# Two attentions on one core: one of four integer patterns moved from VectorE to an accumulating DMA

## The chip, the cores and the metric

The kernel runs on one core of one Trainium2 chip. The metric is the device time of one execution in microseconds, the median of several. PE is TensorE, ACT ScalarE, DVE VectorE, POOL GpSimd and SP SyncE. A run's "granted clock" is the mean share of full speed that TensorE's clock was given. PSUM is the memory that TensorE writes its results to.

## The reference, cut to what matters

```python
def _A_ref(x, wq, wk, wv, wo, beta):       # S = 2048, D = 512, 32 heads of 16, 4 segments of 512
    ...
    for s in range(N):
        logits = einsum('bhqd,bhkd->bhqk', qs, ks) * scale + mask      # causal within the segment
        a_dot = einsum('bhqk,bhkd->bhqd', softmax(logits), vs)
        ...                                                            # plus a memory read, gated
def _B_ref(x, wqkv, wo):                                               # plain attention over all 2048
    scores = einsum('bhqd,bhkd->bhqk', q, k) * Dh ** -0.5
    return einsum('bhqk,bhkd->bhqd', softmax(scores), v) ... @ wo
return concatenate([a, b], axis=-1)
```

B alone has 32 x 2048 x 2048 exponentials; they are the bulk of the work.

## The kernel before

The program is written by a planner in Python. It keeps a clock for each engine and decides, step by step, what TensorE does next; the order that comes out is fixed in the program. Exponentials are made in two ways. ScalarE takes score tiles of two or three banks of 512 columns out of PSUM (`pT`). VectorE takes whole quads: four 128x512 score tiles (four heads, one key block of B). It writes them as 16-bit integers which, read as fp16, are a rough exponential; three more copies with other offsets (the `LADDER`) even out the error, and TensorE adds the four patterns in PSUM.

```python
LADDER = (12914, 13046, 13325, 13628)
VBUFS = 11          # buffers of 128x2048 uint16
VBACK = 1.5         # us of VectorE backlog up to which a score tile for VectorE is added
...
        def v_evac(u, kb, x, j, vt, end):            # first pattern, four times a quad
            def f():
                pin(nc.vector.tensor_scalar(x[:, j, :], vt[:], XSCALE, float(LADDER[0]), ALU.mult, ALU.add))
                if end:
                    buf = [len(LADDER)]
                    v_ready(u, kb, x, buf)
                    for off in LADDER[1:]:
                        later(0.70, v_rung(u, kb, x, off, buf), ...)      # cut
            return f

        def v_rung(u, kb, x, off, buf, pool=False):  # one further pattern, three times a quad
            def f():
                vlive[0] += 1
                p = wk.tile([P, 4, 512], U16, name="vx", tag="vx", bufs=VBUFS)
                ...                                                       # cut
                pin(nc.vector.tensor_scalar(p[:], x[:], float(off - LADDER[0]), 32767.0, ALU.add, ALU.min))
                v_ready(u, kb, p, [1], ...)
                v_done(buf)
            return f
```

ScalarE always takes the next tile; a quad goes to VectorE when buffers, PSUM slots and the backlog allow. So the number of quads is a result of the planning, and ScalarE's number of tiles is what remains.

## Time and profile before

| | before |
|---|---|
| time, median | 897.12 us at the prediction, 897.05 us with one more run |
| profiled span | 893.6 us (of a run of 895.34 us), granted clock 0.996 |
| ACT / PE / DVE busy | 869.0 / 862.0 / 794.3 us |
| exponentials on ACT | 374 of three banks, 375 of two |
| quads on VectorE | 124 (496 evacuations, 372 offsets) |

A group's line in the profile gives the source line, engine, operation, what it writes and reads with shapes, the count, then busy us and mean ns of one, then the idle time of the engine before it and what ended that. The prediction shows the lines of before. Busy time is the union of intervals, so where consecutive instructions overlap, as on ScalarE, it is less than count times mean.

### The profile page before, as it was taken

The numbers are of one execution on the slowest core, as the hardware profiler recorded it, in microseconds if no ns is written. First come the engines' busy times: TensorE is split into PE (matmuls) and PEld (weight loads), VectorE is DVE, ScalarE is ACT, GpSimd is POOL, SyncE is SP. The second block draws the span as 40 slices with busy tenths as digits, with TensorE's granted clock in tenths as the row PEclk, the third lists the DMA queues.
The fourth block names the chain that finished last, engine by engine and source line by source line (L and its number), as shares of the span: only waits on it lengthen the run. The fifth ranks groups of instructions, "written<-read, shape, count | busy, mean of one in ns | idle before, by whom it ended". The sixth has DMA issues, their size and how long they took to land.

```text
span 893.6 us, 18889 instructions
## 1 busy us (share of the span) xinstructions
PE 862.0 (96%) x7659; PEld 258.0 (29%) x7659; DVE 794.3 (89%) x1355; ACT 869.0 (97%) x779; POOL 156.5 (18%) x333
## 2 busy tenths in 40 slices
PE   9999999999999999999999999999999999999996
PEld 3322222332223222232222332223233222222222
DVE  4787689899898897989899998999999999999996
ACT  6999999999999999999999999999999999999995
POOL 5711210430303012040220303003030300000000
PEclk9999999999999999999999999999999999999999
DMA  9400100110002110000000110000000000000000
GB/s 194 89 15 11 67 4 6 30 30 2 5 3 43 37 24 8 1 1 7 2 7 1 47 32 1 2 2 1 1 1 1 7 25 19 1 2 1 1 1 29
DMA packets 42801, 17.05 MB, mean 19 GB/s; under 512 B 34512, under 2 KB 42704, under 8 KB 42704
## 3 DMA queue, kind: packets, MB, share of 16 engines
q1 hardware_dynamic: 41360, 15.23, 7.3%
q8 instruction: 62, 1.02, 0.5%
q10 hardware_dynamic: 1344, 0.52, 0.2%
q14 instruction: 35, 0.29, 0.1%
HBM read 4.20 MB, written 4.19 MB: 9 GB/s over the span
## 4 chain that ended last, share of the span: by engine, by line
PE 28%; ACT 15%; issue 6%; DVE 4%; POOL 1%; ACTq 0%; POOLq 0%
PE acc L117 15%; ACT pT L892 15%; PE s_ps L117 7%; PE v_ps L117 4%; DVE vx L965 1%; DVE vx L981 1%; POOL pT L902 1%; PE o_ps L117 1%; DVE tT L374 0%; PE l_ps L117 0%; PE k_ps L117 0%; ACT ex L299 0%; POOL qB L274 0%; DVE osb L1264 0%; PE q_ps L117 0%
## 5 line engine op out<-in xcount | busy, mean ns | idle before, releaser
L892 ACT ACTIVATE pT<-s_ps 128x1536 bf16<-128x1536 f32 x749 | 856.9, 1286 | 7.2 <-PE s_ps L117 5.4
L965 DVE TENSOR_SCALAR vx<-v_ps 128x512 uint16<-128x512 f32 x496 | 322.9, 682 | 28.4 <-PE v_ps L117 23.6
L117 PE MATMUL s_ps<-qB,KB 32*128 32x512 bf16 x1552 | 251.8, 383 | 10.4 <-ACT pT L892 7.1
L981 DVE TENSOR_SCALAR vx<-vx 128x2048 uint16<-128x2048 uint16 x372 | 244.6, 690 | 4.5 <-PE acc L117 2.6
L117 PE MATMUL acc<-vx,VB 128*32 128x512 f16 x1984 | 178.0, 384 | 1.1 <-DVE vx L981 0.5
L117 PE MATMUL v_ps<-qB,KB 32*128 32x512 bf16 x496 | 175.8, 381 | 2.8 <-DVE KB L253 0.9
L902 POOL TENSOR_SCALAR_AFFINE_SELECT pT<-pT 128x256 bf16<-128x256 bf16 (+2 forms) x241 | 105.7, 473 | 359.4 <-ACT pT L892 358.5
L117 PEld LDWEIGHTS <-KB 32*128 32x128 bf16 x2048 | 83.4, 91 | 245.8 <-issue 238.3
L117 PE MATMUL acc<-pT,VB 128*32 128x512 bf16 x1552 | 151.2, 388 | 0.2 <-DVE tT L374 0.2
L117 PE MATMUL acc<-zeros 128*128 128x512 bf16 x395 | 133.6, 387 | 0.0
L117 PEld LDWEIGHTS <-VB 128*32 128x32 bf16 x3536 | 73.0, 94 | 155.3 <-issue 142.6
L117 PEld LDWEIGHTS <-zeros 128*128 128x128 bf16 x415 | 34.1, 98 | 83.9 <-issue 77.0
L117 PE MATMUL s_ps<-qA,kA 32*128 32x384 bf16 (+3 forms) x512 | 52.6, 299 | 5.0 <-ACT pT L892 2.8
L374 DVE STREAM_TRANSPOSE tT<-acc 128x512 f32<-128x512 f32 x64 | 45.0, 704 | 10.9 <-PE acc L117 10.7
L274 POOL TENSOR_SCALAR qA<-qc,par 128x512 bf16<-128x512 bf16 x24 | 17.4, 739 | 178.7 <-DVE qc L272 178.7
L117 PE MATMUL acc<-pT,vA 128*32 128x256 bf16 (+3 forms) x512 | 32.8, 306 | 1.5 <-DVE vx L965 1.1
L117 PEld LDWEIGHTS <-kA 32*128 32x128 bf16 x512 | 17.7, 91 | 46.1 <-issue 43.3
L454 DVE CAST osb<-o_ps 128x512 bf16<-128x512 f32 x28 | 19.2, 684 | 9.9 <-PE o_ps L117 9.9
L274 POOL TENSOR_SCALAR qB<-qc,par 128x512 bf16<-128x512 bf16 x32 | 23.7, 754 | 11.8 <-DVE qc L272 11.8
L408 POOL TENSOR_TENSOR tN<-tT,rsum 128x512 bf16<-128x512 f32 x1 | 1.4, 1372 | 129.8 <-DVE rsum L397 129.8
L272 DVE CAST qc<-q_ps 128x512 bf16<-128x512 f32 x28 | 19.0, 680 | 2.8 <-PE q_ps L117 2.6
L117 PE MATMUL v_ps<-w_a,xT_a 128*128 128x512 bf16 x64 | 19.3, 384 | 0.3 <-DVE vx L965 0.2
(93 smaller groups left out, 431.6 us busy)
## 6 DMA issues: line engine op xcount, KB each, us to landing
out_dram<-osb SPq DMA_DIRECT2D x30, 128.0 KB, 1.7
w_b<-in_B_wqkv_dram SPq DMA_DIRECT2D x3, 512.0 KB, 6.0
phk<-phkT SPq DMA_TRANSPOSE x48, 2.4
w_a<-in_A_wv_dram SPq DMA_DIRECT2D x1, 512.0 KB, 4.9
wo_a<-in_A_wo_dram SPq DMA_DIRECT2D x1, 512.0 KB, 4.3
wo_b<-in_B_wo_dram SPq DMA_DIRECT2D x1, 512.0 KB, 5.1
xT_b<-in_B_x_dram SPq DMA_TRANSPOSE x28, 3.3
xT_a<-in_A_x_dram SPq DMA_TRANSPOSE x16, 2.8
```

The lines of the kernel that those rows point to most:

```text
L117: return pin(nc.tensor.matmul(out, lhsT, rhs, **k))
L272: pin(nc.vector.tensor_copy(qc[:], ps[:]))
L274: pin(nc.gpsimd.tensor_scalar(dst[:, e, :], qc[:], par[:, e:e + 1], 0.0, ALU.mult, ALU.add))
L374: pin(nc.vector.transpose(st["tT"][:, e].rearrange("p c d -> p (c d)"), acc[:]))
L408: pin(eng.tensor_tensor(o, tT[:, :, :, 0:DH], rr.to_broadcast(bc), op=ALU.mult))
L454: pin(nc.vector.tensor_copy(osb[:], ps[:]))
L892: pin(nc.scalar.activation(pT[:, 0:n, :], pt[:, 0:n, :], ACT.Exp, scale=SCALE))
L902: pin(nc.gpsimd.affine_select(out=blk, in_=blk, compare_op=ALU.is_ge, fill=0.0, base=0, pattern=[[0, len(sls)], [1, P]], channel_multiplie ...
L965: pin(nc.vector.tensor_scalar(x[:, j, :], vt[:], XSCALE, float(LADDER[0]), ALU.mult, ALU.add))
L981: pin(nc.vector.tensor_scalar(p[:], x[:], float(off - LADDER[0]), 32767.0, ALU.add, ALU.min))
```

## The change

The intent: the fourth pattern is the first plus a constant, so after TensorE has used the first pattern and VectorE has made the two others from it, a DMA can add the constant to the first pattern's buffer in place. That takes a third of the offsets from VectorE, and a quad needs one buffer fewer. GpSimd issues the DMA. At the same time there is one buffer more, and a lower backlog limit, and projections of a segment of A are held until the x tiles should have landed.

```diff
-VBUFS = 11
+VBUFS = 12
-VBACK = 1.5
+VBACK = 1.0
+DMARUNG = 3
+ACCPOOL = 1.05
+ACCDMA = 3.0
+ACCLAT = 3.2
+FILL = 2048
...
+        fill = wk.tile([P, 1, FILL], U16, name="fill")
+        nc.gpsimd.memset(fill[:], LADDER[DMARUNG] - LADDER[0])
...
                     chore(d - LEAD, part(q()), 4, after=rel if s else ARRIVE["w1" if rt == 1 else "wq"],
-                          key=("q", "a", s, rt))
+                          key=("q", "a", s, rt), ok=lambda: s in xTA)
...
+                    for c in chores:
+                        if c["key"] in [(w, "a", s, r) for w in "kq" for r in range(NRT)]:
+                            c["after"] = T["sp"] + 4.0
...
-                    buf = [len(LADDER)]
+                    buf = [len(LADDER) - 1, u, kb, x]
...
-                    for off in LADDER[1:]:
-                        later(0.70, v_rung(u, kb, x, off, buf), ...)
+                    for i in range(1, len(LADDER)):
+                        if i != DMARUNG:
+                            later(0.70, v_rung(u, kb, x, LADDER[i], buf), ...)
...
+        def v_sum(u, kb, x):
+            def f():
+                pin(nc.gpsimd.dma_start(out=x[:].rearrange("p j c -> p (j c)").rearrange("p (a c) -> p a c", c=FILL),
+                                        in_=fill[:].to_broadcast([P, 2048 // FILL, FILL]), accum_op=ALU.add))
+                T["dma"] = max(T["dma"], T["pool"]) + ACCDMA
+                v_ready(u, kb, x, [1], T["dma"] + ACCLAT)
+            return f
...
         def v_done(buf):
             buf[0] -= 1
-            vlive[0] -= buf[0] == 0
+            if buf[0] == 0 and len(buf) > 1:
+                atasks.append((max(T["pe"] + PELAT, T["dve"]), v_sum(*buf[1:])))
+            else:
+                vlive[0] -= buf[0] == 0
```

Cut: an unused way to put offsets on GpSimd is removed, the projection of A's keys gets a like condition, `v_done` is called after a pattern's products instead of before them, and the planner's loops drain the waiting sums.

More of the change, by code (lines that the diff above doesn't have):

```diff
@@ L58 @@
 VALONE = 1.4
-POOLMIN = 99
+DMARUNG = 3
[3 more added lines that the diff above has]
+FILL = 2048
 SPLOADS = 38.0
@@ L97, in pin @@
         return tc.keep_in_program_order(ins)
-    T = dict(pe=0.0, act=0.0, dve=0.0, pool=0.0, sp=SPLOADS)
+    T = dict(pe=0.0, act=0.0, dve=0.0, pool=0.0, sp=SPLOADS, dma=0.0)
     group = dict(kind=None, pos=set(), start=0.0, end=0.0)
@@ L138, in on_pool, with later @@
         ports["pool"].append((start, T["pool"]))
-    def later(us, f, src=None, prio=0, ready=None, ok=None, port=False, rung=None):
+    def later(us, f, src=None, prio=0, ready=None, ok=None, port=False):
         if not live[0]:
@@ L146, in later @@
         seq[0] += 1
-        tasks.append(dict(prio=prio, seq=seq[0], ready=ready, us=us, f=f, src=src, ok=ok, port=port, rung=rung))
+        tasks.append(dict(prio=prio, seq=seq[0], ready=ready, us=us, f=f, src=src, ok=ok, port=port))
     def palloc(pool, shape, name):
@@ L578, in project @@
                     chore(d - LEAD, part(k()), 4, after=rel if s else ARRIVE["w1" if rt == 1 else "wk"],
-                          key=("k", "a", s, rt), ok=lambda: s == 0 or ("phk", s - 1, rt) in seen)
+                          key=("k", "a", s, rt), ok=lambda: s == 0 or s in xTA and ("phk", s - 1, rt) in seen)
                     chore(d - LEAD, part(q()), 4, after=rel if s else ARRIVE["w1" if rt == 1 else "wq"],
-                          key=("q", "a", s, rt))
+                          key=("q", "a", s, rt), ok=lambda: s in xTA)
                 if rt == 0:
@@ L687 @@
         held.update(pk=0, ph=0)
-        vlive, npool = [5], [0]
+        vlive = [5]
         def begin(t):
@@ L727, in backlog @@
             return max(0.0, T["dve"] - T["pe"]) + sum(t["us"] for t in runnable() if t["ready"] < T["pe"] + 0.6)
-        ptasks = deque()
+        ptasks, atasks = deque(), deque()
         def in_turn(g, prio, end=None):
@@ L812, in urge @@
             if dve_force():
+                return
+            if atasks:
+                T["pe"] = group["end"] = max(T["pe"], atasks[0][0])
+                pool_run()
                 return
@@ L966, in f, with v_rung @@
                 if end:
-                    buf = [len(LADDER)]
+                    buf = [len(LADDER) - 1, u, kb, x]
                     v_ready(u, kb, x, buf)
-                    for off in LADDER[1:]:
-                        later(0.70, v_rung(u, kb, x, off, buf), prio=2, ready=T["dve"], ok=lambda: vlive[0] < VBUFS,
-                              port=True, rung=v_rung(u, kb, x, off, buf, True) if off == LADDER[1] else None)
+                    for i in range(1, len(LADDER)):
+                        if i != DMARUNG:
+                            later(0.70, v_rung(u, kb, x, LADDER[i], buf), prio=2, ready=T["dve"],
+                                  ok=lambda: vlive[0] < VBUFS, port=True)
             return f
-        def v_rung(u, kb, x, off, buf, pool=False):
+        def v_rung(u, kb, x, off, buf):
             def f():
@@ L977, in f @@
                 p = wk.tile([P, 4, 512], U16, name="vx", tag="vx", bufs=VBUFS)
-                if pool:
-                    pin(nc.gpsimd.tensor_scalar(p[:], x[:], 1.0, float(off - LADDER[0]), ALU.mult, ALU.add))
-                else:
-                    pin(nc.vector.tensor_scalar(p[:], x[:], float(off - LADDER[0]), 32767.0, ALU.add, ALU.min))
-                v_ready(u, kb, p, [1], T["pool"] + 0.4 if pool else None)
-                v_done(buf)
+                pin(nc.vector.tensor_scalar(p[:], x[:], float(off - LADDER[0]), 32767.0, ALU.add, ALU.min))
+                v_ready(u, kb, p, [1])
+                v_done(buf)
+            return f
[5 more added lines that the diff above has]
+                v_ready(u, kb, x, [1], T["dma"] + ACCLAT)
             return f
@@ L993, in pool_run @@
                 f()
-            while T["pool"] < T["pe"] + 0.1:
-                el = [t for t in runnable() if t["rung"] is not None and t["ready"] < T["pe"] + 0.1]
-                if not el or backlog() < POOLMIN:
-                    return
-                t = min(el, key=lambda t: t["seq"])
-                tasks.remove(t)
-                on_pool(2.15, max(T["pe"], t["ready"]))
-                npool[0] += 1
-                t["rung"]()
+            while atasks and (atasks[0][0] < T["pe"] + 0.1 or not live[0]):
+                ready, f = atasks.popleft()
+                T["pool"] = max(T["pool"], ready) + ACCPOOL
+                f()
         def v_ready(u, kb, p, buf, at=None):
@@ L1085, in pv @@
                 pvq.remove(q)
-                if "v" in q:
-                    v_done(q["v"])
                 at = q["ready"]
@@ L1104, in pv @@
                        tile_position=(0, 32 * j), skip_group_check=True)
+                if "v" in q:
+                    v_done(q["v"])
                 if stop:
@@ L1207 @@
                 urge()
-        while chores or cur_chore[0] or tasks or ptasks or len({q["u"]["id"] for q in pvq}) > 1:
+        while chores or cur_chore[0] or tasks or ptasks or atasks or len({q["u"]["id"] for q in pvq}) > 1:
             dve_run(T["pe"])
@@ L1236 @@
             partial(sb, t())
-        while pvq:
+        while pvq or atasks:
+            pool_run()
             assert pv(1, True)
```

## The prediction

> **What bounds the kernel now.** I read the page first (busy shares, then the slices), then the costliest groups, then the waits, then the stretches of time, and last the timeline of the end. The page's busy shares and the slices of PE, DVE and ACT:
>
> ```profile
> PE 862.0 (96%) x7659; PEld 258.0 (29%) x7659; DVE 794.3 (89%) x1355; ACT 869.0 (97%) x779; POOL 156.5 (18%) x333
> ...
> DVE  4787689899898897989899998999999999999996
> ACT  6999999999999999999999999999999999999995
> POOL 5711210430303012040220303003030300000000
> ```
>
> Both ACT and PE look full, but they are not full in the same way. The scores are turned into exponentials on two engines. ACT does it exactly. VectorE takes whole key blocks ("quads" of four 128x512 tiles), evacuates the four as integers (first pattern) and adds three offsets; TensorE sums the four patterns. The costliest groups (operation, tiles, count, then busy us, mean ns of one, idle before):
>
> ```profile
> L892 ACT ACTIVATE pT<-s_ps 128x1536 bf16<-128x1536 f32 x374 | 560.0, 1497 | 7.2 <-PE s_ps L117 5.4
> L892 ACT ACTIVATE pT<-s_ps 128x1024 bf16<-128x1024 f32 x375 | 403.3, 1076 | 0.0
> L965 DVE TENSOR_SCALAR vx<-v_ps 128x512 uint16<-128x512 f32 x496 | 322.9, 682 | 28.4 <-PE v_ps L117 23.6 <-PE s_ps L117 1.6
> L981 DVE TENSOR_SCALAR vx<-vx 128x2048 uint16<-128x2048 uint16 x372 | 244.6, 690 | 4.5 <-PE acc L117 2.6 <-PE v_ps L117 0.3
> L117 PE MATMUL acc<-zeros 128*128 128x512 bf16 x395 | 133.6, 387 | 0.0
> ```
>
> ACT lost only 7.2 us before all its 749 exponentials. PE's 862 us contain 133.6 us of multiplications by zeros, which the schedule puts in where PE would otherwise be idle. So PE has slack that the busy share hides, and ACT has none. The waits say it from the other side: PE waits for ACT more than ACT for PE, and no PE instruction is listed as waiting for an x transfer:
>
> ```profile
> PE s_ps L117 <- ACT pT L892: 9.9, 41, 0.6
> ...
> ACT pT L892 <- PE s_ps L117: 5.4, 15, 0.9
> ```
>
> The busy times of 45 to 880 us (PE, PEld, DVE, ACT, POOL):
>
> ```profile
> 45.00:880.00 835.00, 812.97 (x7291) 241.55 (x7290) 761.72 (x1296) 829.14 (x741) 125.64 (x248) 1.00 0.05 12
> ```
>
> ACT was idle 835.0 - 829.1 = 5.9 us there. The remaining 24.6 - 5.9 = 18.7 us of its idle time lie in the head and in the tail, which no faster VectorE shortens. The kernel is bound by the number of exponentials on ACT; VectorE matters through how many quads it takes from ACT.
>
> **What the Trainium skill says.** First, "DMA: Bandwidth & Descriptors", section "SWDGE vs HWDGE vs iDMA": an accumulating DMA has to be issued from GpSimd, whose cores write the descriptors into SBUF, and VectorE's two-port modes can lock GpSimd out meanwhile. "SBUF — State Buffer", section "Who interferes with whom", names tensor_scalar among the operations that enter those modes, and says that data movement itself does not contend with an engine. The trace of before has no DMA from GpSimd, so it cannot confirm either. Second, "DMA: Bandwidth & Descriptors", section "Anatomy of one DMA": a fit of 2.0 us + bytes / 436 GB/s, which gives 3.2 us for the 512 KB of one tile. The trace is slower for its 512 KB loads, 4.3 to 6.0 us from issue to landing (these come from HBM, partly queued). Third, "Collectives: The Full Stack", section "The bandwidth ceiling: the fold count and why AG ≠ RS ≠ AR": the DMA's add is slow because it reads two sources for one write. No run shows it yet.
>
> **The change, part by part.** Orders of instructions of the two builds, by counting: VectorE's quads go from 124 to 132; evacuations (L965's) 496 to 528; offsets 372 to 264, two a quad; ACT's exponentials from 374+375 to 368+368; accumulating DMAs 0 to 132; zeros 395 to 369.
> - ACT, which sets the end. Durations overlap: 560.0 + 403.3 = 963.3 us of durations are 856.9 us of busy time by the page, so each of the 749 overlaps by 106.4/749 = 0.142 us. One large costs 1.497 - 0.142 = 1.355 us, one small 1.076 - 0.142 = 0.934 us. Saved: 6 x 1.355 + 7 x 0.934 = **14.7 us**, all on the path.
> - VectorE: busy time of one offset 244.6/372 = 0.658, of one evacuation 322.9/496 = 0.651. -108 x 0.658 + 32 x 0.651 = **-50 us**: 794 falls to about 744, some 85% of the new span. It is beside ACT, so it is worth nothing by itself. Of 132 x 0.66 = 87 us freed, only what became eight more quads counts. That is the main reason why I expect little: three quarters of VectorE's work on a quad (four evacuations of about 2.6 us) remains, and the schedule does not fill the rest.
> - PE: each moved quad swaps 4 score tiles for 4 others and 4 value products for 16. By busy time per instruction: +32 x 0.354 (v_ps) - 32 x 0.162 (s_ps) + 128 x 0.090 (vx) - 32 x 0.097 (pT) - 30 x 0.34 (26 zeros and 4 spare ones) = +4 us. The zeros that remain, 369, are about 125 us of slack; PE gets tighter but is not the bound.
> - DMA, mid-kernel: a sum waits for both offsets and for the products of the first pattern, and then its products wait for it. Counting ACT's tiles on PE's order between the release of a sum and its first product, at the two costs above, the smallest distance mid-kernel is 6.9 us and the median 9.2 us (less up to some 1.4 us for the offsets to end). My estimate for a sum, from the page's fit with two reads: 2.0 + 1 MB/436 GB/s = 4.4 us, and about 1 us for descriptors behind VectorE: 5.5 us. So most are hidden. I charge **+2 us** for bursts, where two sums are released 1 to 2 us apart and queue.
> - Tail. Before: the last ACT tile ended at 882.3 and the accumulation at 883.6 us:
>
> ```profile
> 876.73 5.58 ACT L892 ACTIVATE pT<-s_ps 128x1536 bf16<-128x1536 f32 x5
> ...
> 883.18 0.39 PE L117 MATMUL acc<-pT,VB 128*32 128x512 bf16 x4
> ...
> 883.62 0.72 DVE L374 STREAM_TRANSPOSE tT<-acc 128x512 f32<-128x512 f32 x1 [2.00 <-PE acc L117]
> ```
>
> Now the very last product is that of the last sum. By the order its offsets end before the last score tile, so it is released about 2.5 us ahead of ACT's end and lands 5.5 us later, 3 us after ACT; with its products 4 us after, where it was 1.3: **+2.8 us**.
> - Holding the projections of A, twelve buffers for eleven, and one 128x2048 memset: no PE wait for an x tile exists to be removed, and the memset lies in the head on GpSimd. 0 us; the hold is a guard against transfers slowed by the new DMAs.
>
> Sum: 897.1 - 14.7 + 2 + 2.8 = **887.2 us**.
>
> **Rivals.**
> 1. The sums come late. If a sum takes 9 us and not 5.5, about half of the 132 waits are exposed by a microsecond or more, PE works in order, and ACT starves: +30 to +100 us, 920 or slower. For it: three streams a sum, GpSimd behind VectorE's two-port instructions, bursts. Against it: the order keeps at least 6.9 us almost everywhere, and the DMA engines are nearly idle (0.05 from 45 to 880 us).
> 2. The gain arrives whole. If the eight quads cost no new wait, the tail hides, and VectorE at 85% shortens PE's waits for its buffers, the 5.9 us of idle time shrink too: 897.1 - 14.7 - 3 = 879. For it: VectorE was at 94 to 96% from 400 to 800 us. Against it: there is so little idle time on ACT to win, and the tail is plain in the order.
> 3. PE becomes the bound. It was idle 835 - 813 = 22 us mid-kernel, and gets 4 us more work in 15 us less time, leaving about 3 us if no zeros give way. Then ACT waits for scores and half of the saving goes: 890 to 895. For it: PE's high busy share. Against it: zeros are put in only where the schedule has room.
>
> **Range and chances.** The saving on ACT is a count of instructions and the surest term; tail and mid-kernel waits can be 0 to 12 us together. That makes 880 to 896 the likely stretch, with rival 1 above it. Two per cent faster is 879.2, which needs all of rival 2: 0.10. Two per cent slower is 915, which is rival 1 alone: 0.07. Within 2%: 0.83.
>
> **What would show it.** Right: 736 exponentials with unchanged means and about 854 us ACT busy; 264 offsets; VectorE near 744 us; few or no PE waits on DMA except in the tail, where the last accumulation ends 3 to 5 us after ACT's last tile. Wrong: "PE acc <- DMA vx" high in the waits (rival 1); ACT's idle time mid-kernel above some 12 us with PE s_ps as releaser (rival 3), or below 4 us (rival 2); offsets on VectorE longer than 0.69 us, which would be GpSimd holding the shared port.

## The result, and the profile after

The changed kernel took **883.66 us** in the median (883.22 to 884.03, four runs), the kernel before 897.05. The ratio is 0.9843, 95% interval 0.9816 to 0.987: faster by 1.6%, within the 2% that count as the same. Ratios are the mean time of one kernel's runs over that of the other's of the same rounds, so not quite the ratio of the medians quoted. Executions over 1.5% slower than the fastest of the same kernel are left out of the means.

The page's busy shares and three of its slices, after the change:

```profile
PE 853.3 (97%) x7725; PEld 253.6 (29%) x7725; DVE 755.7 (86%) x1280; ACT 854.8 (97%) x766; POOL 269.6 (31%) x466
...
DVE  4778499889898888979989999888979899999994
ACT  6999999999999999999999999999999999999994
POOL 6711402433424134241331414215241411212111
```

ScalarE's row is as full as before, over a span that is 12.1 us shorter (881.5 for 893.6). VectorE lost 38.6 us of work. The costliest groups of the changed kernel, with shapes kept apart:

```profile
L906 ACT ACTIVATE pT<-s_ps 128x1536 bf16<-128x1536 f32 x368 | 550.0, 1495 | 8.4 <-PE s_ps L121 4.9 <-PE v_ps L121 1.3 <-ACT pT L906 0.2
L906 ACT ACTIVATE pT<-s_ps 128x1024 bf16<-128x1024 f32 x368 | 395.1, 1074 | 0.2
L979 DVE TENSOR_SCALAR vx<-v_ps 128x512 uint16<-128x512 f32 x528 | 345.9, 685 | 43.4 <-PE v_ps L121 34.4 <-PE s_ps L121 4.1
L121 PE MATMUL acc<-zeros 128*128 128x512 bf16 x369 | 123.3, 386 | 0.0
L1000 POOL DMA_DIRECT2D vx<-fill x132 | 115.9, 890 | 452.7 <-PE v_ps L121 132.2 <-PE acc L121 114.4 <-DVE vx L979 60.5
L993 DVE TENSOR_SCALAR vx<-vx 128x2048 uint16<-128x2048 uint16 x264 | 173.5, 690 | 2.6
```

Thirteen exponentials fewer, each as long as before (1495 and 1074 ns for 1497 and 1076). The offsets kept their mean of 690 ns. GpSimd now issues 132 DMAs, but in the trace only 9 of these issues overlap an offset by more than 50 ns. What the DMAs cost is in the view of the tile `fill`, the constant:

```profile
L1000 POOL DMA_DIRECT2D vx<-fill x132: 847/859/1372, 72.4 to 865.9; - x132
...
DMA to landing us min/median/max: 4.5/4.9/8.5
```

The first line has the time to issue one (ns, least, median, most), the second the time from issue to landing. In the listed waits of the whole execution TensorE stood still for a sum only once:

```profile
PE acc L121 <- DMA vx<-fill: 1.1, 1, 1.1
```

That one is in the tail. Its timeline (start, length, engine):

```profile
861.58 7.07 ACT L906 ACTIVATE pT<-s_ps 128x1536 bf16<-128x1536 f32 x6
...
865.95 0.86 POOL L1000 DMA_DIRECT2D vx<-fill  x1 [3.08 <-PE acc L121]
...
870.51 0.40 PE L121 MATMUL acc<-vx,VB 128*32 128x512 f16 x4 [1.09 <-DMA vx<-fill]
```

The last exponential ended at 868.65, and the products of the last sum began at 870.51. Now the busy times in the stretch from 45 us to the last exponential and from there to the end, first before, then after (the columns are the stretch, its length, then PE, PEld, DVE, ACT and POOL busy, clock, DMA share, GB/s):

```profile
45.00:882.40 837.40, 815.37 (x7304) 242.42 (x7303) 763.35 (x1298) 831.46 (x743) 125.64 (x248) 1.00 0.05 12
882.40:893.60 11.20, 3.88 (x31) 1.28 (x30) 3.90 (x11) 1.08 (x2) 0.78 (x2) 0.83 0.19 57
```

```profile
45.00:868.70 823.70, 806.96 (x7369) 237.99 (x7370) 725.01 (x1222) 816.81 (x730) 236.61 (x379) 1.00 0.49 96
868.70:881.50 12.80, 3.83 (x34) 1.34 (x25) 3.89 (x11) 1.08 (x2) 0.78 (x2) 0.85 0.26 67
```

This gives the whole account of the two profiles, on ScalarE, which works or idles at every moment (the last stretch has 1.08 us of work in both; its whole length is 11.2 and 12.8 us):

| part of the span | before | after | difference | predicted |
|---|---|---|---|---|
| ACT busy | 869.0 | 854.8 | -14.2 | -14.7 |
| ACT idle, 0 to 45 us | 8.5 | 8.1 | -0.5 | 0 |
| ACT idle, 45 us to the last exponential | 5.9 | 6.9 | +0.9 | +2 |
| ACT idle, last exponential to the end | 10.1 | 11.7 | +1.6 | +2.8 |
| span | 893.6 | 881.5 | -12.1 | -9.9 |

The medians differ by 13.4 us, not by 12.1, because the profile of before is one of that kernel's better runs. In the rounds of the second set of experiments, its eleven runs had spans from 894.1 (clock 0.996) to 898.9 us (clock 0.990); five runs of the changed kernel there had 881.3 to 882.3 at 0.996 to 0.998.

### The profile page after: what moved, and what is told of

It is laid out like the page before. It is cut to its first block, busy times and chain, and to the rows that moved or that the text cites. A ratio compares the mean times of both kernels' runs of the same rounds, so it can differ in the third digit from the quotient of the medians.

```text
span 881.5 us, 19327 instructions
## 1 busy us (share of the span) xinstructions
PE 853.3 (97%) x7725; PEld 253.6 (29%) x7725; DVE 755.7 (86%) x1280; ACT 854.8 (97%) x766; POOL 269.6 (31%) x466
## 4 chain that ended last, share of the span: by engine, by line
PE 34%; ACT 15%; issue 7%; DVE 3%; DMA 1%; POOL 1%; ACTq 0%; POOLq 0%; DVEq 0%
PE acc L121 18%; ACT pT L906 15%; PE s_ps L121 9%; PE v_ps L121 5%; DVE vx L979 1%; DMA vx<-fill 1%; POOL pT L916 1%; DVE vx L993 1%; PE o_ps L121 1%; PE q_ps L121 0%; PE am_ps L121 0%; ACT ex L303 0%; DVE tT L378 0%; PE k_ps L121 0%; PE m_ps L121 0%
## 5 line engine op out<-in xcount | busy, mean ns | idle before, releaser
L906 ACT ACTIVATE pT<-s_ps 128x1536 bf16<-128x1536 f32 x736 | 843.4, 1284 | 8.6 <-PE s_ps L121 4.9
L979 DVE TENSOR_SCALAR vx<-v_ps 128x512 uint16<-128x512 f32 x528 | 345.9, 685 | 43.4 <-PE v_ps L121 34.4
L121 PE MATMUL s_ps<-qB,KB 32*128 32x512 bf16 x1520 | 245.3, 383 | 10.0 <-ACT pT L906 7.2
L1000 POOL DMA_DIRECT2D vx<-fill x132 | 115.9, 890 | 452.7 <-PE v_ps L121 132.2
L121 PE MATMUL v_ps<-qB,KB 32*128 32x512 bf16 x528 | 188.3, 381 | 1.0 <-DVE vx L979 0.5
L121 PE MATMUL acc<-vx,VB 128*32 128x512 f16 x2112 | 185.2, 384 | 2.8 <-DMA vx<-fill 1.1
L993 DVE TENSOR_SCALAR vx<-vx 128x2048 uint16<-128x2048 uint16 x264 | 173.5, 690 | 2.6
L121 PE MATMUL acc<-zeros 128*128 128x512 bf16 x369 | 123.3, 386 | 0.0
L121 PE MATMUL s_ps<-qA,kA 32*128 32x512 bf16 (+3 forms) x512 | 53.1, 300 | 2.8 <-ACT pT L906 1.5
L378 DVE STREAM_TRANSPOSE tT<-acc 128x512 f32<-128x512 f32 x64 | 44.5, 700 | 12.7 <-PE acc L121 12.7
L121 PE MATMUL o_ps<-wo_a,OT_a 128*128 128x512 bf16 x64 | 19.8, 384 | 0.0
```

The source lines that it names most:

```text
L121: return pin(nc.tensor.matmul(out, lhsT, rhs, **k))
L378: pin(nc.vector.transpose(st["tT"][:, e].rearrange("p c d -> p (c d)"), acc[:]))
L906: pin(nc.scalar.activation(pT[:, 0:n, :], pt[:, 0:n, :], ACT.Exp, scale=SCALE))
L1000: pin(nc.gpsimd.dma_start(out=x[:].rearrange("p j c -> p (j c)").rearrange("p (a c) -> p a c", c=FILL), in_=fill[:].to_broadcast([P, 2048 ...
```

## The experiments

Three sets, each with its own runs of the kernel before on the same chip (medians 898.41, 897.16 and 897.05 us). All twelve runs gave correct results. A ratio's 95% interval stands in brackets. "Count" below means exponentials times the two costs of the prediction, 1.355 and 0.934 us: before 857.0, after 842.4 us.

### Which part of the change is it: the two sizes alone (knobs_only)

```diff
 # the kernel before
-VBUFS = 11
+VBUFS = 12
-VBACK = 1.5
+VBACK = 1.0
```

> The kernel before with only the two sizes of the change (12 buffers, backlog limit 1.0), no accumulating DMA. By its build it has 122 quads and 376+376 exponentials. Theory (the time is the count of exponentials on ScalarE plus small terms): 376 x 1.355 + 376 x 0.934 is 3.7 us more than before's, so about 901 us, ratio 1.004. Rival (the gain comes from the buffers and the backlog limit, not from the DMA): about 884 us, ratio 0.985.

Measured: 897.92 us, ratio 0.9992 (0.9976 to 1.0009). The gain doesn't come from the sizes, so the rival falls. The theory is not met to the microsecond either. The profiled span, 896.6 us, is 3.0 above that of before, close to the 3.7 counted; but its four timed runs had a clock of 0.998 where most of before had 0.993, so the medians are equal. In its profile the clock is not lowered before the tail; in that of before it is, once, at 115 us. Why is not shown.

### Is freed VectorE time worth anything without more quads (cap4)

```diff
 # the changed kernel
-                if u["name"] == "a" or len(u["kbs"]) < vmin:
+                if u["name"] == "a" or len(u["kbs"]) < vmin or u.get("nv", 0) >= 4:
                     continue
```

> The changed kernel with at most four quads in a unit: 121 quads, all with the sum by DMA, 377+376+1 exponentials, so VectorE has far less to do than in either kernel (242 offsets for 372). Theory (VectorE's relief is worth only the quads made of it): 5.5 us more on ScalarE than before and 1.6 us of tail, about 904 us, ratio 1.008. Rival (VectorE was itself on the path, its relief shortens waits): clearly below before, 890 us or less.

Measured: 898.12 us, ratio 0.9997 (0.9981 to 1.0014). The right comparison is knobs_only, which has the same sizes: 121 quads against 122, a count 1.8 us higher, and a time 0.2 us higher, while VectorE was busy for 715.2 us against 790.9. So 76 us less work on VectorE, without quads made of it, bought at most some 2 us. The absolute value was again expected too high, as in knobs_only.

### The old sizes with the DMA (old_knobs)

```diff
 # the changed kernel
-VBUFS = 12
+VBUFS = 11
-VBACK = 1.0
+VBACK = 1.5
```

> The changed kernel with the two sizes of before (11 buffers, backlog limit 1.5): 135 quads, 366+365 exponentials, 5.6 us less on ScalarE than in the changed kernel. Theory of the count: about 878 us, ratio 0.979. Rival (with fewer buffers and a deeper backlog TensorE waits longer, ScalarE idles): the saving is given back, 884 us or more, with the idle time of ScalarE before its exponentials well above 8.6 us.

Measured: 891.70 us, ratio 0.9921 (0.9904 to 0.9938), clock 0.989 to 0.992. The count fell, and the time rose by 8 us over the changed kernel's: the rival of the expectation holds. The idle time before the exponentials was 18.5 us. Much of the loss is at one place. Its timeline around 110 us:

```profile
108.20 1.85 POOL L916 TENSOR_SCALAR_AFFINE_SELECT pT<-pT 128x384 bf16<-128x384 bf16 x5 [0.40 <-ACT pT L906]
...
110.00 0.84 POOL L1000 DMA_DIRECT2D vx<-fill  x1
...
114.50 0.62 PE L121 MATMUL acc<-vx,VB 128*32 128x512 f16 x4 [4.44 <-DMA vx<-fill]
```

The sum stood in GpSimd's queue behind causal masks of A and was issued at 110.00, directly after them. TensorE waited 4.44 us for it. The queue is only part of the cause: by the trace the products of the first pattern, which the sum has to wait for, ended at 108.77, so the masks held it back by some 1.2 us. The rest is that this order had put the products of the sum only some 1.3 us behind those of the first pattern, while a sum needs 4.5 us to land. In the ten microseconds after 115 us the granted clock was 0.74 and ScalarE was busy for 5.9 of 10:

```profile
115.00:125.00 10.00, 9.60 (x63) 2.40 (x55) 6.39 (x10) 5.87 (x6) 0.29 (x1) 0.74 0.04 15
```

A lowered clock after such a pause is what the Trainium skill says in "TensorE: Matmul & The Clock Gate", section "What's actually happening": a monitor lowers the clock when TensorE has been idle for a window of about 3.4 us. The trace agrees here: the clock was 0.5 for 6.83 us from 113.32 us, within the wait. But other traces have the lowered clock without such a pause. In the profile of the kernel before, TensorE was busy for 2.55 of the 3.50 us ahead of it, with no pause over 0.63 us:

```profile
111.40:114.90 3.50, 2.55 (x29) 0.91 (x26) 3.46 (x7) 3.50 (x4) 0.29 (x1) 1.00 0.02 5
114.98:118.39 3.41, 3.38 (x16) 0.58 (x15) 3.20 (x8) 2.79 (x3) 0.00 (x0) 0.50 0.00 0
```

So a pause of a whole window is not needed; the measurement decides. What share of work suffices was not measured.

### The hold of A's projections (no_hold)

```diff
 # the changed kernel
-                          key=("k", "a", s, rt), ok=lambda: s == 0 or s in xTA and ("phk", s - 1, rt) in seen)
+                          key=("k", "a", s, rt), ok=lambda: s == 0 or ("phk", s - 1, rt) in seen)
-                          key=("q", "a", s, rt), ok=lambda: s in xTA)
+                          key=("q", "a", s, rt))
-                    for c in chores: ...          # the new "after" of these chores
```

> The changed kernel without the hold of A's projections; 132 quads, the same 368+368 exponentials, eight zeros fewer. Theory (a guard only, the x tiles land in time anyway): 884 us, ratio 0.985, no wait of TensorE on xT_a. Rival (transfers slowed by the sums make TensorE wait for x tiles): one or more waits on xT_a, 1 to 4 us each, 885 to 890 us.

Measured: 883.15 us, ratio 0.9838 (0.9813 to 0.9863). No wait of TensorE on an x tile is in the trace; these transposes landed in 2.6 to 4.5 us (median 2.8), as before. The second half of the change is worth nothing measurable here.

### The tail (tail_vector, beside after_again)

> The changed kernel once more, for comparison with the others on the same chip: 883.7 us, ratio to before 0.984, granted clock 0.997 or so.

Measured: 883.29 us, ratio 0.984 (0.9823 to 0.9856).

```diff
 # the changed kernel
-                    buf = [len(LADDER) - 1, u, kb, x]
+                    tail = u["id"] == len(units) - 1 and len(u["kbs"]) < 4
+                    buf = [len(LADDER)] if tail else [len(LADDER) - 1, u, kb, x]
-                        if i != DMARUNG:
+                        if tail or i != DMARUNG:
```

> The changed kernel, but the very last quad's third offset is done by VectorE again (131 sums by DMA, 265 offsets, the same 368+368 exponentials). Theory (the last sum lengthens the tail by 1.6 us): from the end of the last exponential to the end of the span 11.2 us as before the change, not 12.8; 882.1 us, ratio 0.982. Rival (the tail is bound by the outputs, not by the accumulation): 12.8 us, 883.7 us.

Measured: 882.64 us against 883.29, ratio 0.9831 (0.9815 to 0.9847). In its profile the last exponential ended at 860.10 + 9.32 = 869.42 and the span at 880.7, so the tail is 11.3 us, as before the change (12.7 us in after_again). The mechanism holds in the profile. The medians gain 0.65 and not 1.6 us, and the single times of the two overlap (882.40 to 883.35 and 883.03 to 884.12); in its profile the last eight exponentials began 0.8 us later than in after_again's (860.10 for 859.33), which explains part of it.

### More quads (back2)

```diff
 # the changed kernel
-VBACK = 1.0
+VBACK = 2.0
```

> The changed kernel with the backlog limit of VectorE at 2.0 instead of 1.0: 137 quads, 364+364 exponentials, 9.2 us less on ScalarE. Theory of the count alone: 874.5 us, ratio 0.973. Rival (seen with 11 buffers and limit 1.5: a deep backlog makes sums and evacuations late, TensorE stops, its clock is lowered and ScalarE starves): 882 us or more, clock below 0.995, idle time before the exponentials 15 us or more.

Measured: **877.48 us**, ratio 0.9775 (0.9759 to 0.9792), beating both kernels. The count fell by 9.2 us and the time by 5.8. The idle time before the exponentials was 9.6 us, near the changed kernel's 8.6. The tail grew to 14.7 us (from 854.07 + 6.91 to 875.7), with the last sums behind each other:

```profile
857.34 0.92 POOL L1000 DMA_DIRECT2D vx<-fill  x1 [4.08 <-PE s_ps L121]
...
859.31 0.86 POOL L1000 DMA_DIRECT2D vx<-fill  x1 [1.04 <-PE s_ps L121]
...
864.74 0.40 PE L121 MATMUL acc<-vx,VB 128*32 128x512 f16 x4 [2.32 <-DMA vx<-fill]
```

So the reading of old_knobs, that a deeper backlog as such makes sums late, falls: with 12 buffers a limit of 2.0 works.

### VectorE's time given back, order unchanged (busy_vector)

```diff
 # the changed kernel, in v_rung
+                for _ in range(1 + (off == LADDER[2])):
-                pin(nc.vector.tensor_scalar(p[:], x[:], float(off - LADDER[0]), 32767.0, ALU.add, ALU.min))
+                    pin(nc.vector.tensor_scalar(p[:], x[:], float(off - LADDER[0]), 32767.0, ALU.add, ALU.min))
```

> The changed kernel, order unchanged, but VectorE executes one of the two offsets of each quad twice (396 offsets, 132 sums): VectorE gets its 87 us back and stands at about 843 us, 95% of the span. Theory (freed VectorE time is worth only the quads it is turned into): at most 3 us more, 884 to 887 us. Rival (VectorE's slack itself keeps TensorE's waits short): ScalarE idles 10 us more, 894 us or more, ratio 0.995.

Measured: 948.10 us, ratio 1.058 (1.0543 to 1.0616). My theory as I had put it falls clearly. 85 us more on VectorE (840.7 for 755.7 busy) cost 65 us of time. The profile is of a slower run (952.61 us), whose clock was lowered for 13.65 us at 335 us. In its waits:

```profile
ACT pT L906 <- PE s_ps L121: 44.0, 100, 1.2
PE v_ps L121 <- DVE vx L979: 22.5, 56, 1.1
...
ACT pT L906 <- PE v_ps L121: 14.6, 33, 1.0
PE acc L121 <- DVE vx L994: 12.5, 32, 0.8
```

TensorE waits for VectorE's evacuations and offsets 0.4 us at a time, and ScalarE in turn for TensorE. VectorE was idle for 14% of the span, but in an order that is fixed around its planned instructions that idle time could not take up an instruction that the planner does not know of. This doesn't contradict cap4: there the planner knew what VectorE had to do, and without more quads nothing came of it.

### Late sums (late_sums)

```diff
 # the changed kernel: half the constant in fill, and twice
-        nc.gpsimd.memset(fill[:], LADDER[DMARUNG] - LADDER[0])
+        nc.gpsimd.memset(fill[:], (LADDER[DMARUNG] - LADDER[0]) // 2)
+                for _ in range(2):
-                pin(nc.gpsimd.dma_start(...))
+                    pin(nc.gpsimd.dma_start(...))
```

> The changed kernel, order of TensorE, VectorE and ScalarE unchanged, but each sum is made of two accumulating DMAs of half the offset, the second waiting for the first: the result is the same and the last of it lands some 5 us later, 10 to 11 us after its release where the order leaves 6.9 us at the least and 9.2 us in the median. Theory (the sums are hidden by a margin of only 2 to 4 us): most of the 132 waits of TensorE show, 1 to 3 us each, its clock is lowered, ScalarE starves: 940 to 1000 us. Rival (there is more slack than counted): under 900 us.

Measured: 1395.11 us, ratio 1.5556 (1.5524 to 1.5587), clock 0.761. The direction is the theory's; the loss of 512 us is over four times even the largest that I had expected (1000 - 883 = 117). Its waits:

```profile
PE acc L121 <- DMA vx<-fill: 300.6, 107, 6.9
ACT pT L906 <- PE s_ps L121: 261.9, 151, 5.8
ACT pT L906 <- PE v_ps L121: 204.3, 103, 6.7
```

The waits are as long as expected, 300.6/107 = 2.8 us, so 107 of 132 sums were late. The span of this profile is 506.4 us longer than that of the changed kernel, and the waits are 301 of them. I had left out the lowered clock (0.72 from 300 to 400 us, for example): TensorE was busy for 1052.2 us with the instructions that took 853.3 in the changed kernel, 199 us more (with 58 records missing), and the mean of a product with `vx` rose from 384 to 474 ns. These two terms leave some 7 us. I had also left out GpSimd, whose queue stood still for 520.1 us waiting for the first DMA of each pair, with masks behind it: the second DMA was issued 6.9 us after the first (median) and landed 11.5 us after the first was issued, so the sums were 6.6 us later and not 5. How much of the waits that queue made was not separated.

### Eleven buffers alone (bufs11)

```diff
 # the changed kernel
-VBUFS = 12
+VBUFS = 11
```

> The changed kernel with 11 buffers instead of 12, backlog limit 1.0 as in the change: 130 quads, 370+369 exponentials, 3.6 us more on ScalarE than with 12. Theory (the twelfth buffer is worth only its two quads): 887 us, ratio 0.988. Rival (with 11 buffers sums and offsets get in each other's way, as with 11 buffers and limit 1.5): above 889 us, with waits of TensorE for a sum and a clock below 0.995.

Measured: 892.86 us, ratio 0.9951 (0.9935 to 0.9966), clock 0.991 to 0.994. That is 9.6 us slower than the changed kernel, of which 3.6 are the count. The cause that I had named, late sums, is not there (1.3 us of waits). The trace shows another one at 546 us:

```profile
544.36 5.32 POOL L916 TENSOR_SCALAR_AFFINE_SELECT pT<-pT 128x384 bf16<-128x384 bf16 x13
...
545.75 4.48 DVE L993 TENSOR_SCALAR vx<-vx 128x2048 uint16<-128x2048 uint16 x2
...
550.88 0.58 PE L121 MATMUL v_ps<-qB,KB 32*128 32x512 bf16 x1 [3.64 <-DVE vx L979]
```

Two offsets took 4.48 us where 1.29 is usual; the longest offset of this run is 3654 ns, against 934 in the changed kernel. It coincides with thirteen masks in a row on GpSimd, of which nine overlap the longest offset. Then TensorE waited 3.64 us, the granted clock from 550 to 560 us was 0.72, and ScalarE lost 5.1 us from 540 to 560. This fits the lock-out that the prediction quoted from "SBUF — State Buffer", here with GpSimd's masks holding VectorE up; the trace shows the coincidence and not the lock. It recurs: offsets beside five masks took 2148 and 2082 ns in deep_tail, and one beside ten took 3510 ns in late_sums. That eleven buffers must lead to such a place is not shown; the order is another one, and it fell this way.

### Deeper still (deep_tail)

```diff
 # the changed kernel, with the tail of tail_vector for the last two quads (len(u["kbs"]) < 6)
-VBACK = 1.0
+VBACK = 3.0
```

> Backlog limit 3.0 and the last two quads' third offsets on VectorE: 139 quads, 137 sums, 362+363 exponentials, 12.8 us less on ScalarE than the changed kernel and 3.6 us less than with the limit at 2.0. If the count goes on ruling and the tail shrinks by 2 us: 872 us, ratio 0.972. Rival (the deeper backlog makes sums late, as one wait of 2.3 us and 4.3 us of ScalarE's waits for v_ps with the limit at 2.0 hint): 877 us or more.

Measured: 888.54 us (883.15 to 891.74), ratio 0.9901 (0.9873 to 0.9929), clock 0.986 to 0.991. The rival's number holds, but not its reason: 12.8 us of count were saved and more than that given back, with 20.3 us of idle time before the exponentials. From 125 to 145 us the clock was 0.83 and ScalarE busy for 14.4 of 20 us. Sums were not the cause (2.1 us of waits); `ACT pT <- PE v_ps` had 11.2 us. The timeline shows what set it off:

```profile
120.10 4.92 SPq L334 DMA_TRANSPOSE phk<-phkT  x4
...
125.12 3.05 SPq L460 DMA_DIRECT2D out_dram<-osb  x4
...
127.12 0.69 DVE L458 CAST osb<-o_ps 128x512 bf16<-128x512 f32 x1 [3.43 <-DMA out_dram<-osb]
...
127.87 0.37 PE L121 MATMUL v_ps<-qB,KB 32*128 32x512 bf16 x1 [1.83 <-DVE osb L458]
```

The output tiles of A have three buffers. Their DMAs stood in SyncE's queue behind four transposes, VectorE waited 3.43 us for a free buffer, TensorE 1.83 us for VectorE, and from 128.75 us the clock was 0.5 for 6.83 us. The trigger is again a queue that is served in order; that a limit of 3.0 must lead to it is not shown. The profile is of one of the two fastest of six runs (883.24 us), so what cost the median run 5 us more was not seen.

### The kernel before once more (before_again)

> The kernel before once more for a second profile, as most of its runs have a granted clock of 0.993 and a span of some 896.6 us where the first profile has 0.996 and 893.6 us. Expected: 898 us, the same counts, and a lowered clock and idle time on ScalarE in one or two slices between 100 and 200 us.

Measured in one look: 894.90 us, span 893.2 us, clock 0.996, and the counts, busy times and idle time of ScalarE of the first profile (869.0 us busy, 7.1 us idle before the exponentials). It fell on a good run again, so what lowers the clock further in the others was not seen. From 100 to 200 us its clock was 0.98, as in the first profile: one stretch of 3.41 us at 0.5, from 114.4 us (from 115.0 in the first).

## Why the prediction was right

The time, 883.7 us, lies within the range of 880 to 896, the class is the one given 0.83, and the predicted 887.2 was 3.5 us too high.

- **ScalarE's count.** Right. 14.7 us predicted, 14.2 measured on all of ScalarE and 856.9 - 843.4 = 13.5 on the exponentials alone, with unchanged means. That the count rules is shown by back2, where it rules again with a loss at the tail. It does not rule alone: old_knobs and deep_tail have a lower count and are slower.
- **VectorE.** The -50 us of the working were -38.6 in the profile. The two groups behaved as worked out (offsets 244.6 to 173.5, evacuations 322.9 to 345.9, together -48.1); the rest is that neighbouring instructions of different groups overlap, by 48.9 us in all before and 38.9 after. The "three quarters of VectorE's work on a quad" that remain are wrong by the working's own costs: (2.60 + 1.32)/(2.60 + 1.97) is 86%. The words "it is beside ACT, so it is worth nothing by itself" are right for planned work (cap4 against knobs_only, 76 us for at most some 2) and wrong as a statement on slack: busy_vector.
- **TensorE.** The +4 us were mis-sized. Its busy time fell by 8.7 us. The same rows after the change give +12.5 for v_ps, -6.5 for s_ps, +7.2 for vx, -4.0 for pT and -11.7 for zeros and spares, -2.5 in all; I had charged the products with their old busy time each, and more of them overlap now. The other 6 us of the fall are not assigned. So rival 3, which rested on PE being left with 3 us, had no ground: it was idle 823.7 - 807.0 = 16.7 us mid-kernel.
- **Sums mid-kernel.** Hidden, as predicted; the +2 us charged for bursts did not come. No wait of TensorE for a sum is listed mid-kernel. That ScalarE's idle time there grew by 0.9 us, not far from 2, is luck and not this term: its waits for `v_ps`, none before, make up 1.3 us, and those for `s_ps` fell. The estimate was 5.5 us for a sum; measured are 4.9 us from issue to landing (up to 8.5), against distances of 6.9 us and more in the order. The 1 us in it for descriptors behind VectorE was too much, as few issues overlap an offset. The danger of rival 1 was real and near: late_sums, with sums landing 11.5 us after their issue and GpSimd's queue blocked as well, lost 512 us, where I had put 30 to 100 for sums of 9 us.
- **Tail.** Right in kind, 1.6 us for 2.8. The last sum was issued 2.7 us before ScalarE's end, as worked out, but its landing took 4.5 us and not 5.5. The accumulation then ended 2.3 us after ScalarE's last tile, where it was 1.3 and I had put 4. So 1.0 of the 1.6 us is the sum's; 0.5 lies after the last output DMAs were issued (5.1 us to the end before, 5.7 after).
- **The hold and the buffer.** The hold is 0 (no_hold). The twelfth buffer, which I had put at 0, is worth 9.6 us in this change (bufs11), 3.6 of them by quads. The sizes on the old kernel are worth nothing (knobs_only), and the DMA with the old sizes only half (old_knobs, 6.7 us): the parts work together.
- **The remaining terms.** ScalarE idled 0.5 us less in the first 45 us, which I had not forecast. Another 1.3 us are that before's median run was slower than its profiled one. I had taken the difference between median and span, 3.5 us, over to the new kernel as it stood; there it is 883.66 - 881.5 = 2.2.

## What to carry to other kernels

Work taken from an engine that is not the bound pays only through what the planner puts in its place: count the bounding engine's instructions in both builds before believing in the freed time. When a result comes by DMA into a fixed order, compare its landing time with the least distance the order leaves, and look at what else stands in the queue of the engine that issues it. A single wait of TensorE can cost more than its length: in old_knobs, bufs11 and deep_tail waits of 4.4, 3.6 and 1.8 us went with a clock of 0.5 for 6.83 us, and ScalarE lost 8.7, 5.1 and 5.6 us in the 20 us around them. So the best setting is not the one with the lowest count, and it has to be tried on the chip.

## What the Trainium skill lacked or had wrong

- "DMA: Bandwidth & Descriptors" gives no duration for an accumulating DMA. Here one of 512 KB in SBUF took 0.86 us of GpSimd to issue and landed 4.5 / 4.9 / 8.5 us after the issue began (least, median, most). The page's fit with the bytes counted twice, an estimate of 4.4 us, came close. No run has the same DMA without the add, so the prediction's reason, two sources for one write, is not tested.
- The same page warns that VectorE's two-port modes lock GpSimd out while it writes descriptors, and gives no size. In the changed kernel 9 of 132 issues overlapped an offset by more than 50 ns; they took 1169 ns (median) where the others took 859, and five of the nine ended 85 or 86 ns after the end of an offset. So the trace agrees, and the cost is some 0.3 us for the few that meet.
- "SBUF — State Buffer" says that the second to issue is blocked until the other instruction finishes. In bufs11 an offset of 0.69 us took 3.65 us while nine GpSimd masks ran one after another, 0.41 us each (5.32/13): the wait went on over several instructions, not one. In eleven traces offsets beside at most one mask took 0.69 us (median), beside three 1.03, beside five 1.99. No page has it.
- "TensorE: Matmul & The Clock Gate" has the clock lowered after at least one idle window of about 3.4 us. Here the lowered stretches are 0.5 and last 3.41 us or multiples of it outside the tail, as the page has it, but a whole idle window is not needed: in the profile of the kernel before TensorE was busy for 2.55 of the 3.50 us ahead, and in deep_tail its longest pause was 1.83 us.
